# Loading k and v of batches 2 to 7 from ScalarE's DMA queue in place of SyncE's

## The chip, the cores and the metric

The kernel runs on one core of a Trainium2 chip. The metric is the device time of one execution in microseconds (us). The engines are named as in the profile: PE is TensorE's matmul side and PEld its weight loading, DVE is VectorE, ACT ScalarE, POOL GpSimd and SP SyncE. SP computes nothing here; it issues DMAs. A DMA that ACT issues stands in ACT's own instruction stream, between its activations, and goes into a queue of ACT's own; both queues are worked off by the same 16 DMA engines of the core.

## The reference

```python
# q, k, v: (8, 8, 576, 64) float32   g_norm: (64,)   w_in: (512, 2048)   w_out: (2048, 512)
kv = np.einsum('bhsd,bhse->bhde', k, v)
out = np.einsum('bhsd,bhde->bhse', q, kv)
rms = np.sqrt(np.mean(out * out, axis=-1, keepdims=True) + 1e-06)
x = (out / rms * g_norm).transpose(0, 2, 1, 3).reshape(8 * 576, 8 * 64)
h = x @ w_in
result = (h * np.cos(h)) @ w_out      # (4608, 512)
```

So for each batch and head, k and v make one 64 x 64 matrix `kv`; q times `kv`, normalized, gives the rows of `x`; and all 4608 rows go through two large matmuls with `h * cos(h)` between them.

## The kernel before

**Tiling.** The 4608 tokens are cut into 9 chunks of 512. A batch has 576 tokens, so chunks and batches overlap: batch b feeds chunk b - 1 and chunk b, roughly. Float32 matmuls are made of three passes over numbers split into a high and a low part (tiles ending in `hi` and `lo`, halves of `wi` and `wo`). Chunks 0 to 2 go through 48 steps, each with one 128-column block of `w_in` (12 matmuls into a `bank`) and the matching 128 rows of `w_out` (12 matmuls into four `acc` banks). Chunks 3 to 8 go in pairs through "quads" (`quad_part`, L1483): seven products of sums and differences take the place of eight, with weights read back from the DRAM tensors `wq` (for `w_in`) and `wod` (for `w_out`), which the kernel wrote earlier. In the profile those read-backs are the 512 KB loads `wo<-wq` and `wo<-wod`; `wo` is also the name of the buffers of w_out's split, in which they land.

**k and v.** Batches 0 and 1 (FRONT = 2) are loaded at the start in a way of their own. For each later batch b:

- `kv_loads` (L562) loads, for each of four pairs of heads, 512 of the 576 tokens of k into a tile `m` and of v into a tile `sg`, 256 KB each. `m` and `sg` come in five slots, which other stages use too.
- `over_loads` (L570) loads the last 64 tokens of all heads into `k_over` and `v_over`, 128 KB each.
- `kv_part` (L758) multiplies them on PE: the matmuls `bank<-sg,m` and `bank<-v_over,k_over`, pair after pair. ACT and DVE then split the result into `kv_w` (casts `kv_w<-bank` on ACT).
- `x_part` (L892) multiplies q by `kv_w` and normalizes. q comes through small DMAs `qb<-in_q_dram`, up to eight to a pair of heads.

That makes ten loads to a batch, of which six batches are concerned: 60 DMAs. Batch 2's are spread from 113 to 159 us; those of batches 3 to 7 come in bursts from 164, 213, 352, 364 and 423 us.

**What sets the order.** The class `Order` (L55) plays the whole program through when it is built, with costs and due times (`due`, L320, and the table `haste`, L327), and every instruction is recorded in the order in which it is chosen there; `Pinned` (L231) keeps that order on each engine. `dmas` (L520) takes 0.5 us of SP for an issue in this planner, whichever engine then issues, and allows eight DMAs in flight (`t_fly`, L513).

**Semaphores of DMAs.** In the built program the DMAs of all queues take eight semaphores in turn, `DMAHW0` to `DMAHW7`, and each DMA waits at its issue until the DMA before it on the same semaphore has landed, unless another wait already covers that. An engine that issues a DMA stands at that wait with all that follows in its stream.

**Places that the prediction speaks of.** The tiles `m`, `sg`, `k_over`, `v_over`; the weight loads `wo<-wq`; ACT's chain for h times cos(h) (`chain_part`, L1559: an activation into `ki`, DVE, a sine on ACT, DVE), and in the quads the adds that finish a bank (`add`, L1519; `snap`, L1513: copies `wi<-bank`).

Of the kernel before, what the change touches and what calls it, by code (L numbers as in the profile page):

```python
# [20 lines left out]
P = 128  # L21
# [164 lines left out]
def tile_kernel(  # L186
# [11 lines left out]
    B, H, S, D = q.shape  # L198
# [9 lines left out]
    SI = S // P  # L208
    ST = S - SI * P
# [31 lines left out]
    pe, act, dve, pool, sp = (Pinned(x) for x in (nc.tensor, nc.scalar, nc.vector, nc.gpsimd, nc.sync))  # L241
# [78 lines left out]
    def due(i):  # L320

        t = 24.0 + STEP * min(i, NS) + 2.0 * min(i, 11)
        first = max(0, min(i - NS, QUAD * NM))
        return t + 3.9 * first + 5.2 * max(0, i - NS - QUAD * NM)
# [136 lines left out]
    def put_off(*key):  # L461
        return haste.get(key, 0.0)
# [20 lines left out]
    def chunks_of(b):  # L483
        return [c for c in range(NCH) if any(x[0] == b for x in chunk_parts(c))]
# [26 lines left out]
    DMA_LAT, STORE_LAT = 1.3, 0.7  # L511
# [17 lines left out]
        yield "wait", landed  # L529
        return max(e.t for e in landed)  # L530

    def copies(out, in_, us, late=DMA_LAT):
        return us, late, lambda: sp.dma_start(out=out, in_=in_)

    def stores(out, in_, us):
        return copies(out, in_, us, STORE_LAT)
# [22 lines left out]
    def two(slot, shape, dtype, which):  # L559
        return at.tile(shape, dtype, name=f"{('m', 'sg')[which]}{slot}", bufs=1)  # L560

    def kv_loads(b, p):  # L562
        def pieces(slot):
            kv_tiles[b, p] = [two(slot, [P, 2, SI, D], F32, n) for n in range(2)], slot
            return [
                copies(t, src[b, 2 * p:2 * p + 2, 0:SI * P, :].rearrange("h (p i) d -> p h i d", i=SI), 0.74)
                for t, src in zip(kv_tiles[b, p][0], (k, v))]
        return pieces

    def over_loads(b):  # L570
        def pieces():
            return [
                copies(t[0:ST], src[b, :, SI * P:S, :].rearrange("h p d -> p h d"), 0.75)
                for t, src in ((k_over, k), (v_over, v))]
        return pieces

# [525 lines left out]
    def window(c):  # L1102

        if c < PLAIN:
            first = last_step[c - 2] + 1
            return first, begin[c] - first
        two_chunks, half = divmod(c - PLAIN, 2)
        first, n = (NS + QUAD * NM * (two_chunks - 1), QUAD * NM) if two_chunks else (begin[PLAIN - 1] - 4, NJ)
        return first + half * n // 2, n // 2
# [519 lines left out]
    for c in range(FRONT):  # L1629
        for p in range(NP):  # L1630
            t = due(begin[c]) - 32 + 3 * p if c else -100.0 + p
# [16 lines left out]
    for c in range(FRONT):  # L1648
        for p in range(NP):
            t = due(begin[c]) - 24 + 1 * p if c else -10.0 + 0.5 * p  # L1650
# [3 lines left out]
    for key in sorted(need, key=lambda x: (need[x], x)):  # L1654
        t = due(need[key]) - 14.0 + put_off("load", *key)
# [12 lines left out]
    for b in range(FRONT, B):  # L1668
        i, _ = window(chunks_of(b)[0])
# [8 lines left out]
    for c in range(FRONT, NCH):  # L1678
        first, n = window(c)
        for p in range(NP):  # L1680
            i, late = (first - 3 + p * (n - 1) // NP, 4) if c < PLAIN else (first + p * n // NP, 4 if c < PLAIN + 2 else 7)
# [9 lines left out]
    for j in range(NJ):  # L1691
        i = KEEP + j * (NS - KEEP - 8) // NJ
# [4 lines left out]
    for m in range(NM):  # L1697
        i = SUMS + m * (NS - SUMS - 6) // NM
# [46 lines left out]
```

## Time and profile before

| | |
|---|---|
| three timed runs | 840.77, 842.40 (median), 845.24 us |
| the profiled execution | 844.05 us, of which the span is 842.20 us |
| granted PE clock over the span | 0.997 |
| PE, PEld busy | 825.9 us (98%), 681.1 us (81%) |
| DVE, ACT, POOL busy | 613.8 us (73%), 498.2 us (59%), 227.6 us (27%) |
| moved by DMA | 181.20 MB, mean 215 GB/s |
| queue q1 (SP's) | 179.68 MB, 69.0% of the 16 engines' span |
| queue q10 (ACT's) | 0.72 MB, 0.2% |

How to read what is quoted: a row of a timeline gives start, duration, engine, line, operation, out<-in, shapes and a count (of merged instructions, with the duration of the whole stretch), and in brackets the engine's idle time before it and what ended that. Nearly all rows have line L239, the helper that records every instruction, so tiles' names tell them apart. "SPq" and "ACTq" are DMA issues by the sequencers of SP and ACT. A row of the DMA view gives the tile, the issuing queue, the count, the size, and the median time from issue to landing. A row of waits gives the waiting engine and tile, what it waited for, and us in total, times, longest. A row of stretches has the busy time of each engine with its count of instructions, then PE's clock, the DMA engines' mean busy share and GB/s. In the DMA view, a queue's row gives packets, MB and share of the 16 engines' time.

### The profile page before, as it was taken

Reading aid. Unit: us, or ns where it says so; the run is one execution under the profiler, and the core shown is the slowest. Engines: PE = TensorE matmul, PEld = TensorE weight load, DVE = VectorE, ACT = ScalarE, POOL = GpSimd, SP = SyncE. Lnnn points to the kernel's source line nnn. Section 1 sums busy time; section 2 is a strip of 40 time slices with the busy share of each in tenths; the row PEclk is TensorE's granted clock in tenths of the full one; section 3 lists DMA queues with packets and bytes.
Section 4 is the critical chain, followed back from the end, with each engine's and each line's share of the span. In section 5 each row is a group of like instructions: output and inputs, shape, how many; then the busy total and the mean of one; then the engine's idle time right before and its main releaser. Section 6 shows DMA issues by size and latency. Waiting matters only on the chain.

```text
span 842.2 us, 12749 instructions
## 1 busy us (share of the span) xinstructions
PE 825.9 (98%) x4424; PEld 681.1 (81%) x4424; DVE 613.8 (73%) x963; ACT 498.2 (59%) x974; POOL 227.6 (27%) x150
## 2 busy tenths in 40 slices
PE   8799999999999999999999999999999999999998
PEld 7678888888888887888887888888788888888886
DVE  3999994469598878669999968878899575444221
ACT  4879983445265565557786657767675464444321
POOL 3310034724427762010324620122438000000000
PEclk9999999999999999999999999999999999999999
DMA  9997535665765577598898767777557566763664
GB/s 301 299 399 275 176 113 190 194 176 155 236 184 189 152 205 269 175 335 254 267 278 233 216 190 183 211 248 201 176 200 240 175 195 191 229 215 105 223 206 145
DMA packets 150399, 181.20 MB, mean 215 GB/s; under 512 B 73920, under 2 KB 113600, under 8 KB 150336
## 3 DMA queue, kind: packets, MB, share of 16 engines
q1 hardware_dynamic: 149824, 179.68, 69.0%
q8 instruction: 35, 0.57, 0.3%
q10 hardware_dynamic: 512, 0.72, 0.2%
q14 instruction: 28, 0.23, 0.1%
HBM read 143.66 MB, written 36.70 MB: 214 GB/s over the span
## 4 chain that ended last, share of the span: by engine, by line
PE 81%; DMA 8%; DVE 5%; ACT 3%; issue 1%; SPq 1%; POOL 0%; DVEq 0%; ACTq 0%; POOLq 0%
PE bank L239 42%; PE acc L239 40%; DMA wi<-in_q_dram 2%; DVE r L239 1%; DMA wo<-wq 1%; DMA x<-slot 1%; DMA out_dram<-slot 1%; DMA wi<-in_v_dram 1%; DVE slot L239 1%; ACT slot L239 1%; DMA sg<-in_v_dram 1%; DMA slot<-part 1%; SPq L239 1%; DVE glo L239 1%; DMA wq<-slot 1%
## 5 line engine op out<-in xcount | busy, mean ns | idle before, releaser
L239 PE MATMUL acc<-wo,ghi 128*128 128x512 f32 x1152 | 355.7, 390 | 1.3 <-ACT slot L239 1.3
L239 PEld LDWEIGHTS acc<-wo,ghi 128*128 128x128 f32 x1152 | 215.4, 188 | 46.3 <-ACT slot L239 2.2
L239 PE MATMUL bank<-wi,wo 128*128 128x512 f32 (+2 forms) x1092 | 244.2, 380 | 4.2 <-DMA wo<-wq 2.0
L239 PEld LDWEIGHTS bank<-wi,wo 128*128 128x128 f32 (+2 forms) x1092 | 191.8, 185 | 46.8 <-DVE glo L239 2.4
L239 PE MATMUL acc<-wo,glo 128*128 128x512 f32 x576 | 224.3, 389 | 0.0
L239 POOL TENSOR_TENSOR rinv<-ms,mhalf 128x16 f32<-128x16 f32 (+1 forms) x36 | 97.2, 2703 | 228.9 <-DVE ms L239 228.5
L239 PEld LDWEIGHTS acc<-wo,glo 128*128 128x128 f32 x576 | 108.1, 188 | 23.0
L239 PE MATMUL bank<-xhi,wi 128*128 128x512 f32 x320 | 99.8, 393 | 0.2 <-DVE slot L239 0.2
L239 DVE TENSOR_TENSOR wi<-bank,wi 128x512 f32<-128x512 f32 x72 | 49.5, 687 | 44.4 <-PE bank L239 35.9
L239 DVE TENSOR_TENSOR glo<-wo,ghi 128x512 fp32r<-128x512 f32 x58 | 42.5, 732 | 46.1 <-ACT ghi L239 45.8
L239 ACT ACTIVATE ki<-wi 128x512 int32<-128x512 f32 x72 | 45.1, 627 | 42.4 <-DVE wi L239 33.7
L239 PEld LDWEIGHTS bank<-xhi,wi 128*128 128x128 f32 x320 | 58.8, 188 | 13.5 <-DVE r L239 0.8
L239 ACT CAST ghi<-wo 128x512 fp32r<-128x512 f32 x61 | 37.8, 619 | 48.4 <-PE acc L239 47.8
L239 ACT ACTIVATE ki<-bank 128x512 int32<-128x512 f32 x72 | 42.6, 591 | 34.2 <-PE bank L239 29.4
L239 PE MATMUL bank<-xlo,wi 128*128 128x512 f32 x160 | 62.4, 390 | 0.0
L239 ACT COPY wi<-bank 128x512 f32<-128x512 f32 x72 | 41.9, 583 | 24.2 <-PE bank L239 23.6
L239 ACT ACTIVATE wo<-wo 128x512 f32<-128x512 f32 x61 | 38.4, 630 | 26.1 <-DVE wo L239 25.8
L239 DVE TENSOR_TENSOR glo<-r,ghi 128x512 fp32r<-128x512 f32 x60 | 44.0, 733 | 13.1 <-ACT ghi L239 10.6
L239 ACT ACTIVATE r<-r 128x512 f32<-128x512 f32 x60 | 37.8, 630 | 20.1 <-DVE r L239 19.6
L239 DVE SCALAR_TENSOR_TENSOR r<-bank,ki 128x512 f32<-128x512 f32 x51 | 34.8, 683 | 19.9 <-ACT ki L239 19.4
L239 ACT CAST ghi<-r 128x512 fp32r<-128x512 f32 x60 | 37.1, 618 | 17.4 <-PE acc L239 16.0
L239 DVE TENSOR_TENSOR r<-r,bank 128x512 f32<-128x512 f32 x51 | 34.5, 678 | 8.5 <-ACT r L239 8.4
(175 smaller groups left out, 1071.6 us busy)
## 6 DMA issues: line engine op xcount, KB each, us to landing
wo<-wod SPq DMA_DIRECT2D x96, 512.0 KB, 3.4
wo<-wq SPq DMA_DIRECT2D x84, 512.0 KB, 4.0
out_dram<-slot SPq DMA_DIRECT2D x35, 256.0 KB, 3.4
wo<-in_moe_w_out_dram SPq DMA_DIRECT2D x16, 512.0 KB, 9.6
wi<-in_moe_w_in_dram SPq DMA_DIRECT2D x16, 512.0 KB, 9.9
wod<-wo SPq DMA_DIRECT2D x16, 512.0 KB, 4.1
wq<-wi SPq DMA_DIRECT2D x24, 256.0 KB, 3.5
m<-in_k_dram SPq DMA_DIRECT2D x24, 256.0 KB, 4.4
```

The source lines that it names most:

```text
L239: return lambda *a, **kw: tc.keep_in_program_order(f(*a, **kw))
```

## The change

`copies` can be told which engine issues, and the loads of `kv_loads` and `over_loads` name ACT:

```diff
-    def copies(out, in_, us, late=DMA_LAT):
-        return us, late, lambda: sp.dma_start(out=out, in_=in_)
+    def copies(out, in_, us, late=DMA_LAT, engine=None):
+        return us, late, lambda: (engine or sp).dma_start(out=out, in_=in_)
...
-                copies(t, src[b, 2 * p:2 * p + 2, 0:SI * P, :].rearrange("h (p i) d -> p h i d", i=SI), 0.74)
+                copies(t, src[b, 2 * p:2 * p + 2, 0:SI * P, :].rearrange("h (p i) d -> p h i d", i=SI), 0.74, engine=act)
...
-                copies(t[0:ST], src[b, :, SI * P:S, :].rearrange("h p d -> p h d"), 0.75)
+                copies(t[0:ST], src[b, :, SI * P:S, :].rearrange("h p d -> p h d"), 0.75, engine=act)
```

The planner still counts the issue on SP. The order of the instructions of PE, DVE and POOL is the same, and so is that of all that stays on ACT and on SP. What moves is where the 60 issues stand, and with it which DMA comes before which on the eight semaphores. The place that matters most below is batch 5, in the first quads.

On SP, this is the program before, from one weight load to the next; `wo_4010` and `wo_4042` are two of the 512 KB loads, between them stand batch 5's ten loads:

```order
L239 DMA wo_4010<-wq 128x1024 [waits DMAHW6_49,PE_49]
L239 DMA k_over<-in_k_dram 64x8x64 [waits DMAHW3_49]
L239 DMA m_4023<-in_k_dram 128x2x256 [waits DMAHW4_49]
L239 DMA m_4025<-in_k_dram 128x2x256 [waits DMAHW5_49]
L239 DMA m_4027<-in_k_dram 128x2x256
L239 DMA m_4029<-in_k_dram 128x2x256 [waits DMAHW7_49]
L239 DMA v_over<-in_v_dram 64x8x64 [waits DMAHW0_49]
L239 DMA sg_4024<-in_v_dram 128x2x256 [waits DMAHW1_49]
L239 DMA sg_4026<-in_v_dram 128x2x256 [waits DMAHW2_49]
L239 DMA sg_4028<-in_v_dram 128x2x256 [waits DMAHW3_49]
L239 DMA sg_4030<-in_v_dram 128x2x256 [waits DMAHW4_49]
L239 DMA wo_4042<-wq 128x1024 [waits DMAHW5_49,PE_49]
```

And the same place on SP with the change:

```order
L239 DMA wo_4010<-wq 128x1024 [waits DMAHW6_49,PE_49]
L239 DMA wo_4042<-wq 128x1024 [waits DMAHW0_49,PE_49]
L239 DMA wo_4070<-wq 128x1024 [waits DMAHW3_49,DMAHW1_49,PE_49]
L239 DMA wo_4082<-wq 128x1024 [waits DMAHW6_49,PE_49]
L239 DMA wo_4109<-wq 128x1024 [waits DMAHW2_49,DMAHW4_49,DMAHW0_49,PE_49]
L239 DMA wo_4129<-wod_146 128x1024 [waits DMAHW1_49,PE_49]
```

The ten loads are gone from SP, and the weight loads follow each other directly. Of their semaphores, some now belong to loads that ACT issues: `wo_4109` waits with DMAHW0 for `m_4029`.

On ACT, the same ten loads in the difference (+ is what the change adds), from the copy into `wi` on; the row of `k_over` stands just above it:

```order
+L239 DMA m_4023<-in_k_dram 128x2x256
+L239 DMA m_4025<-in_k_dram 128x2x256
+L239 DMA m_4027<-in_k_dram 128x2x256 [waits DMAHW7_49]
+L239 DMA m_4029<-in_k_dram 128x2x256 [waits DMAHW0_49]
 L239 ACTIVATE ki<-wi_3517 128x512 [waits DVE_49,Activation_49]
+L239 DMA v_over<-in_v_dram 64x8x64 [waits DMAHW1_49]
+L239 DMA sg_4024<-in_v_dram 128x2x256 [waits DMAHW2_49]
+L239 DMA sg_4026<-in_v_dram 128x2x256 [waits DMAHW4_49]
+L239 DMA sg_4028<-in_v_dram 128x2x256 [waits DMAHW6_49,DMAHW5_49]
 L239 ACTIVATE wo_3383<-wo_3383 128x512 [waits DVE_49]
+L239 DMA sg_4030<-in_v_dram 128x2x256 [waits DMAHW7_49]
 L239 ACTIVATE ki<-wi_3642 128x512 [waits Activation_49]
```

`sg_4026`, `sg_4028` and `sg_4030` now wait on ACT until `m_4023`, `m_4025` and `m_4027` have landed, and the activations into `wo_3383` and from `wi_3642` stand behind them.

## The prediction, made before the change was run

> **What bounds the kernel now.** I read the page first, then who waits for whom from 113 us on, where the moved loads begin, then the timelines of SP, PE and ACT around each batch of loads.
>
> ```profile
> span 842.2 us, 12749 instructions
> PE 825.9 (98%) x4424; PEld 681.1 (81%) x4424; DVE 613.8 (73%) x963; ACT 498.2 (59%) x974; POOL 227.6 (27%) x150
> ...
> PE bank L239 <- DMA wo<-wq: 2.0, 1, 2.0
> PE acc L239 <- ACT slot L239: 1.3, 2, 1.2
> PE bank L239 <- DVE r L239: 0.4, 2, 0.2
> ```
>
> TensorE works 98% of the span. From 113 us on it waits for five things, these three rows and two smaller ones, so for 2.0 + 1.3 + 3 x 0.4 = 4.5 us at most, and never for k or v. So nothing that frees SP can win more than 4.5 us. The 2.0 us wait is for a weight load that no moved load stands near, which leaves 2.5 us. A loss has no such bound: every microsecond by which ACT or a k/v load comes too late for TensorE is paid in full.
>
> **The change: ACT's time.** Sixty loads leave SP: 48 into m and sg, 12 into k_over and v_over.
>
> ```profile
> L239 SPq DMA_DIRECT2D m<-in_k_dram x24: 372/462/1702, 128.0 to 434.2; - x24
> L239 SPq DMA_DIRECT2D k_over<-in_k_dram x6: 601/604/717, 112.9 to 425.5; - x6
> ...
> 1.73 1.28 ACT L239 ACT_TABLE_LOAD   x1 [1.73 <-issue]
> 1.80 0.53 ACTq L239 DMA_DIRECT2D gcol<-in_g_norm_dram  x1
> ```
>
> An issue takes SP 0.46 us (0.60 for the two "over" tiles). The one issue of ACT's shown here took 0.53, much the same, so ACT's sequencer gets 48 x 0.46 + 12 x 0.60 = 29 us more, beside 498 us of busy time in 842. It ran at 1.80, inside the table load of 1.73 to 3.01: one issue between two activations hides behind the first of them. I take nothing for a single one (from 0 up to 0.46 if not hidden), and 0.5 for each further one in a row.
>
> **The change: the early batches (2, 3, 4) and 7.** Batches 3, 4 and 7 are loaded far ahead of their matmuls; batch 4 stands for them, with the last pairs of batch 2.
>
> ```profile
> 213.29 2.80 SPq L239 DMA_DIRECT2D m<-in_k_dram  x3
> 262.02 0.69 PE L239 MATMUL bank<-sg,m 128*64 128x64 f32 x16 [0.17 <-DVE r L239]
> ...
> sg<-in_v_dram SPq DMA_DIRECT2D x1, 256.0 KB, 4.4
> 159.41 0.62 ACT L239 CAST sg<-slot 128x512 fp32r<-128x512 f32 x1 [0.83 <-POOL slot L239]
> 164.51 0.64 PE L239 MATMUL bank<-sg,m 128*64 128x64 f32 x16
> ```
>
> With 262.02 - 213.29 = 49 us to go, batch 4's landings cannot matter. ACT's delay can: two or three issues in a row, between activations, put it 0.5 to 1.5 us back, mostly caught up in its idle time. I choose 0.2 us for batches 3 and 4 together (0 to 0.7) and, as ACT is busier there, 0.4 us for batch 7 (0 to 1.0). Batch 2's last v load now stands behind a cast that waits for POOL until 159.41. Issued at 159.45, it lands at 159.45 + 4.4 = 163.9, 0.6 before its matmul at 164.51: nothing, and up to 0.5 if the cover fails.
>
> **The change: batch 5, where it is decided.** Here the loads are issued at 352 and multiplied at 363.
>
> ```profile
> 351.73 0.32 SPq L239 DMA_DIRECT2D wo<-wq  x1
> 352.10 0.60 SPq L239 DMA_DIRECT2D k_over<-in_k_dram  x1
> 352.75 2.15 SPq L239 DMA_DIRECT2D m<-in_k_dram  x4
> 354.94 0.61 SPq L239 DMA_DIRECT2D v_over<-in_v_dram  x1
> 355.60 2.36 SPq L239 DMA_DIRECT2D sg<-in_v_dram  x4
> 357.49 0.47 SPq L239 DMA_DIRECT2D sg<-in_v_dram  x1
> 358.06 3.56 SPq L239 DMA_DIRECT2D wo<-wq  x4
> k_over<-in_k_dram SPq DMA_DIRECT2D x1, 128.0 KB, 4.5
> sg<-in_v_dram SPq DMA_DIRECT2D x1, 256.0 KB, 5.9
> wo<-wq SPq DMA_DIRECT2D x1, 512.0 KB, 6.6
> wo<-wq SPq DMA_DIRECT2D x1, 512.0 KB, 8.0
> 363.24 0.69 PE L239 MATMUL bank<-sg,m 128*64 128x64 f32 x16
> 365.04 0.64 PE L239 MATMUL bank<-sg,m 128*64 128x64 f32 x16
> 368.58 0.61 PE L239 MATMUL bank<-wi,wo 128*128 128x512 f32 x2
> 356.00:360.00 4.00, 4.00 (x20) 3.30 (x19) 3.26 (x6) 1.84 (x4) 0.00 (x0) 1.00 1.10 310
> ```
>
> The DMA rows give issue to landing. k_over lands at 352.10 + 4.5 = 356.6, the last sg (the row of 357.49 shows it alone) at 357.49 + 5.9 = 363.4. The first of the four 512 KB weight loads behind them lands at 358.06 + 6.6 = 364.7, the fourth, whose issue of 0.32 ends the stretch at 358.06 + 3.56 = 361.62, at 361.30 + 8.0 = 369.3: one every (369.3 - 364.7) / 3 = 1.5 us. The last row is a stretch of 4 us; its last but one column, a DMA share of 1.10, says that the engines are full, so landings follow the queue's order. The last pair of k and v is multiplied at 365.04: its cover is 1.6 us. The first weight load is used only at 368.58, 3.9 us after it lands. SP's single queue put the urgent loads ahead of the patient ones.
>
> The change takes that order away. What SP now issues after 351.73 is the next weight load.
>
> ```profile
> SPq L239 <- DMA m<-in_k_dram: 1.4, 2, 1.1
> 350.63 10.64 PE L239 MATMUL bank<-wi,wo 128*128 128x512 f32 x46
> q1 hardware_dynamic: 383, 0.38, 53.8%
> q10 hardware_dynamic: 191, 0.40, 51.8%
> ```
>
> Before, two of those loads waited for k loads to land (first row, SP's waits from 351.9 to 362). Their other wait is for TensorE to leave a weight buffer: two products of six matmuls at 10.64 / 46 = 0.23 us, so about 2.8 us after 351.73, at 354.5. So the first goes out some 3.5 us earlier, ahead of most v loads. The last two rows are 3 to 5 us, the only time when both queues have work: q1 (SP's) moves 0.38 MB, q10 (ACT's) 0.40 MB. Two full queues share evenly. While k and v go on (6.8 us from first to last landing), SP's queue gets as much again, as far as it has loads: three for certain (due at about 354.5, 357.3 and 360), a fourth once the fourth m load has landed. By landing order the last sg comes at 363.4 + n x 1.5: 367.9 with n = 3, 369.4 with n = 4. TensorE is ready at 365.04, so it loses 2.9 or 4.4 us. I take 3.4, three loads and a third of the fourth; the ends are 0.9 (only one gets by: 363.4 + 1.5 = 364.9, but then ACT's own lateness counts, below) and 4.4.
>
> [...]
>
> ACT is late there too. Each DMA waits until the one eight before it has landed; on ACT, that holds back the activations behind it.
>
> ```profile
> m<-in_k_dram SPq DMA_DIRECT2D x2, 256.0 KB, 4.5
> m<-in_k_dram SPq DMA_DIRECT2D x1, 256.0 KB, 5.8
> 357.80 0.61 ACT L239 ACTIVATE ki<-wi 128x512 int32<-128x512 f32 x1
> 361.33 0.69 DVE L239 TENSOR_TENSOR wo<-wo,bank 128x512 f32<-128x512 f32 x1
> ```
>
> The m loads need 4.5 to 5.8 us. The third went out on SP at about 353.9 (third of four in 2.15 us from 352.75); on ACT, behind a cast and a copy, I estimate 354.7, and a landing near 359.6; only then may the last sg go, and behind it stands the activation that began at 357.80: it starts at 360.0, 2.2 late. It heads a chain through DVE and ACT that ended at 361.33 + 0.69 = 362.0 and that TensorE needs at 363.24, so 1.2 of it is covered and 1.0 is lost, up to 2.5 if sharing holds that m load up by another 1.5. It ends in the same stretch of TensorE as the missing sg, so the two do not add: the larger, 3.4, counts. Without sharing this 1.0 is what is left.
>
> **The change: batch 6.** Loaded at 364 to 376 and multiplied far later. With TensorE 3.4 us late, what ACT waits for has mostly landed when it asks: 0.
>
> **Sum.** 3.4 + 0.2 + 0.4 = 4.0 us. The profiled execution took 844.05 us (span 842.20), so 848.05 for it; the median of the three runs is 842.40, 1.65 below, so I forecast 842.4 + 4.0 = **846.4 us**. A difference under 0.5%, 4.2 us, can hardly be told from none in this kernel: the three runs reach from 840.77 to 845.24.
>
> **The rivals.**
> *The cover holds.* Sharing costs the v loads little, one weight load gets by, and ACT's lateness of 1.0 is all. For it: the weight loads may start more slowly than I think. Against it: 53.8% and 51.8% on the two queues. With batch 7's share or without, 1.0 to 1.5 us: 843.5 us.
> *ACT's waits run on through batch 6 (the other side: clearly slower).* There, two copies and a chain of casts stand behind an sg load that, by the eight-apart rule, waits for a q load.
>
> ```profile
> 366.33 0.88 SPq L239 DMA_DIRECT2D qb<-in_q_dram  x1
> qb<-in_q_dram SPq DMA_DIRECT2D x1, 40.0 KB, 8.0
> 370.14 0.59 ACT L239 COPY wi<-bank 128x512 f32<-128x512 f32 x1 [0.71 <-PE bank L239]
> ```
>
> It landed at 366.33 + 8.0 = 374.3, so with an issue of 0.4 the copy of 370.14 would start at 374.8, 4.6 late. It decides once that exceeds the copy's cover before TensorE; if SP's loads shift along with TensorE, so that batch 5's 3.4 gives no relief, and there is no cover, it is 4.0 + 4.6: 851.0 us. For it: SP's own queue now waits for ACT's loads. Against it: SP, rid of ten issues, sends that q load no later.
> *Faster.* SP's freed time removes what is left of TensorE's waits: 842.4 - 2.5 = 839.9 us. Against it: those waits are for ACT and DVE, not for SP.
>
> **How the numbers follow.** The forecast's case (2.5 to 6 us lost) has 0.48, the cover that holds 0.27, the run-on 0.20, faster 0.05. The forecast's case alone is 844.9 to 848.4. To hold 8 in 10 the range goes down over the second case, less the scatter of a median, to 842.0, and up to 850.0, leaving out the worst of the run-on. Slower by over 0.5% (above 846.6) is the run-on's 0.20 and 0.22 of the forecast's 0.48: 0.42. Faster by over 0.5% needs more than the 2.5 us there are: 0.03 for scatter. The same: 0.55.
>
> **What would show it.** In the profile of the changed kernel: the weight load wo<-wq issued near 354.5 and not at 358; TensorE idle for some 3 us before one of the bank<-sg,m groups near 365, released by a DMA from in_v; the sg loads of batch 5 taking 7 to 10 us; activations at 357 to 361 some 2 to 4 us late. The forecast is wrong if that stop is under 1 us (the v loads kept their place), or if TensorE stops again at 370 to 385 behind ACT.

## The result, and the profile after

| | before | changed |
|---|---|---|
| median of six runs | 842.42 us (840.77 to 845.24) | 851.29 us (849.86 to 852.83) |
| profiled execution | 844.05 us | 852.83 us |
| ratio of the times | | 1.0101, 95% interval 1.0087 to 1.0115 |

The change costs 8.9 us. The forecast was 846.4 us with a range up to 850.0: the direction and the place were right, the size was not.

First the head of the page of the changed kernel, and of TensorE's waits from 113 us on the four rows that are new or longer (waiting engine and tile, what it waited for, us in total, times, longest).

```profile
span 851.0 us, 12722 instructions
PE 829.0 (97%) x4424; PEld 682.5 (80%) x4424; DVE 614.4 (72%) x963; ACT 497.9 (59%) x974; POOL 228.4 (27%) x150
...
PE bank L239 <- DMA sg<-in_v_dram: 3.2, 2, 2.2
PE bank L239 <- DVE wo L239: 1.4, 1, 1.4
PE bank L239 <- DVE sg L239: 0.9, 2, 0.6
PE bank L239 <- DVE wi L239: 0.7, 1, 0.7
```

TensorE waits for a v load, which it never did before, and it is also 829.0 - 825.9 = 3.1 us longer busy with the same 4424 matmuls. The stops for v are all at batch 5, and the matmuls there take 3.2 us longer; what they gain and lose elsewhere cancels to about nothing. The timelines of SP and ACT there:

```profile
351.18 10.21 SPq L239 DMA_DIRECT2D wo<-wq  x5
362.80 0.32 SPq L239 DMA_DIRECT2D wo<-wod  x1
...
352.83 2.31 ACTq L239 DMA_DIRECT2D m<-in_k_dram  x4
355.93 3.30 ACTq L239 DMA_DIRECT2D sg<-in_v_dram  x3
359.28 0.63 ACT L239 ACTIVATE wo<-wo 128x512 f32<-128x512 f32 x1 [3.41 <-DMA m<-in_k_dram]
359.57 0.38 ACTq L239 DMA_DIRECT2D sg<-in_v_dram  x1
359.99 0.63 ACT L239 ACTIVATE ki<-wi 128x512 int32<-128x512 f32 x1
```

SP now issues its weight loads without a break, five wo<-wq from 351.18 to 361.39 and a wo<-wod at 362.80. ACT stands 3.41 us at the issue of an sg load until an m load has landed, with the activations behind it. In the DMA view, first the last sg load and the wo<-wod load, each looked up alone (last column: us from issue to landing), then the two queues from 363 to 368 us (packets, MB, share of the 16 engines' time):

```profile
sg<-in_v_dram ACTq DMA_DIRECT2D x1, 256.0 KB, 10.7
wo<-wod SPq DMA_DIRECT2D x1, 512.0 KB, 7.2
...
q1 hardware_dynamic: 435, 1.53, 75.1%
q10 hardware_dynamic: 520, 0.50, 28.4%
```

The sg load lands at 359.57 + 10.7 = 370.3 and the wo<-wod load at 362.80 + 7.2 = 370.0: all five loads that SP issued behind 351.18 got past it. The numbers of packets are not far apart here, but SP's average 3.5 KB (1.53 MB in 435) and ACT's 1.0 KB (0.50 MB in 520), so SP got three times the bytes. What TensorE did then, from its timeline and from the table of stretches (the third column from the end is its granted clock):

```profile
364.20 0.69 PE L239 MATMUL bank<-sg,m 128*64 128x64 f32 x16 [1.44 <-DVE wo L239]
368.06 1.12 PE L239 MATMUL bank<-sg,m 128*64 128x64 f32 x16 [2.20 <-DMA sg<-in_v_dram]
370.42 1.12 PE L239 MATMUL bank<-sg,m 128*64 128x64 f32 x16 [1.02 <-DMA sg<-in_v_dram]
373.13 1.05 PE L239 MATMUL acc<-wo,ghi 128*128 128x512 f32 x2
375.22 0.61 PE L239 MATMUL acc<-wo,ghi 128*128 128x512 f32 x2
...
366.00:368.00 2.00, 0.00 (x0) 0.00 (x0) 1.97 (x4) 1.46 (x3) 0.00 (x0) 0.96 1.03 400
368.00:370.00 2.00, 1.33 (x20) 1.15 (x20) 0.74 (x2) 0.00 (x0) 0.00 (x0) 0.50 0.62 139
372.00:374.00 2.00, 2.00 (x6) 1.52 (x6) 1.10 (x2) 1.04 (x3) 0.00 (x0) 0.50 0.44 137
```

Three stops, 1.44 + 2.20 + 1.02 = 4.7 us, the first behind ACT and DVE, the other two for v. After the two microseconds without a matmul the clock is granted at half, and the same two matmuls that take 0.61 us at 375 take 1.05 at 373.

As the instructions of TensorE stand in the same order in every kernel here, the same matmul can be looked up in two traces. The table gives how much later than in the first profile of the kernel before TensorE stands after a stretch than ahead of it; the columns name the times in that profile. The kernels are those of the experiments below.

| us gained (-) or lost (+) between | start, 45 | 110, 245 (batches 2 to 4) | 330, 345 | 345, 382 (batches 5, 6) | 432, 470 (batch 7) | end |
|---|---|---|---|---|---|---|
| changed | +0.3 | +1.4 | -2.6 | **+7.9** | +1.6 | +8.8 |
| changed, second profile | +0.3 | +0.4 | -3.0 | **+7.8** | +1.9 | +7.4 |
| before, second profile | +1.2 | +0.2 | -2.4 | 0.0 | 0.0 | -0.3 |
| batch 5 on ACT | +0.5 | -0.6 | -3.6 | **+8.4** | -0.5 | +4.4 |
| all but batch 5 on ACT | +1.7 | 0.0 | -2.3 | +1.0 | +3.5 | +3.8 |
| batch 5 on POOL | +5.0 | 0.0 | -2.6 | 0.0 | -0.5 | +2.5 |
| batch 5 on ACT, weights in 1 KB runs | +2.1 | +0.1 | -2.8 | **+4.4** | -1.0 | +3.1 |
| k of batch 5 on ACT, three profiles | -0.5, +5.0, +0.4 | -0.8, -0.2, -0.1 | -2.8, -2.7, +0.1 | **+2.5, +2.7, +2.8** | -0.6, +0.2, -0.3 | -2.0, +5.3, +2.8 |
| v of batch 5 on ACT | +1.3 | -0.5 | -3.0 | **+7.1** | -0.6 | +4.8 |
| batch 7 on ACT | +2.0 | +0.1 | -2.9 | 0.0 | +0.9 | +0.5 |
| batches 2, 3, 4, 6 on ACT | +0.2 | +0.3 | -2.4 | +0.2 | -0.6 | -2.4 |

The first column and the third are scatter of single executions: the program is the same up to some 350 us in the kernels that move batch 5 or 7 alone (with POOL up to 331 us, where its first load stands). The third column is negative because the first profile of the kernel before had a stop there that hardly any other had (below). The column of batch 5 repeats within 0.1 us for the changed kernel and within 0.3 for k alone, and carries the result.

### The profile page after: what moved, and what is told of

Same layout as the page of the kernel before. It is cut to its first block, busy times and chain, and to the rows that moved or that the text cites. A ratio compares the mean times of both kernels' runs of the same rounds, so it can differ in the third digit from the quotient of the medians.

```text
span 851.0 us, 12722 instructions
## 1 busy us (share of the span) xinstructions
PE 829.0 (97%) x4424; PEld 682.5 (80%) x4424; DVE 614.4 (72%) x963; ACT 497.9 (59%) x974; POOL 228.4 (27%) x150
## 4 chain that ended last, share of the span: by engine, by line
PE 77%; DMA 8%; DVE 6%; ACT 4%; POOL 2%; issue 1%; SPq 1%; ACTq 0%; DVEq 0%; POOLq 0%
PE acc L239 39%; PE bank L239 38%; DMA sg<-in_v_dram 2%; DMA wq<-m 2%; DVE r L239 1%; DMA m<-in_k_dram 1%; DMA x<-slot 1%; POOL m L239 1%; POOL rinv L239 1%; DVE sg L239 1%; ACT slot L239 1%; DVE glo L239 1%; DMA wq<-wi 1%; DMA qb<-in_q_dram 1%; ACT ghi L239 1%
## 5 line engine op out<-in xcount | busy, mean ns | idle before, releaser
L239 DVE TENSOR_TENSOR glo<-r,ghi 128x512 fp32r<-128x512 f32 x60 | 44.4, 739 | 13.2 <-ACT ghi L239 10.6
```

Source lines behind the costliest of these rows:

```text
L239: return lambda *a, **kw: tc.keep_in_program_order(f(*a, **kw))
```

## The experiments

The theory after the result: TensorE's loss is made at batch 5, where (a) SP's weight loads, in runs of 4 KB, pass ACT's k and v loads, in runs of 1 KB, because the two queues share by packets and not by bytes (a guess that fits 435 packets to 520 above, and that the runs below test), and (b) the granted clock halves behind the stops (0.50 at 368 to 374 above). The rivals: ACT's waits for landings hold its activations back, and that makes TensorE late; or the sixty issues cost ACT a little everywhere.

Medians in us, each kernel beside the kernel before on the same chip. The ratio is worked out from all runs and is not that of the two medians; where it is turned into us below, it is taken times the median before. The second looks at the end are single executions and not in the table:

| kernel | median | before, same chip | ratio, 95% interval |
|---|---|---|---|
| batch 5 on ACT | 850.86 | 843.72 | 1.0092 (1.0067 to 1.0118) |
| all but batch 5 on ACT | 845.14 | 843.72 | 1.0032 (1.0012 to 1.0052) |
| batch 5 on POOL | 844.74 | 843.72 | 1.0025 (1.0008 to 1.0042) |
| batch 5 on ACT, weights in 1 KB runs | 846.48 | 843.72 | 1.0044 (1.0025 to 1.0062) |
| k of batch 5 on ACT | 846.60 | 843.35 | 1.0034 (1.0012 to 1.0056) |
| v of batch 5 on ACT | 849.52 | 843.35 | 1.0069 (1.0052 to 1.0086) |
| batch 7 on ACT | 844.46 | 843.35 | 1.0017 (1.0000 to 1.0034) |
| batches 2, 3, 4, 6 on ACT | 844.53 | 843.35 | 1.0012 (0.9994 to 1.0029) |

### Batch 5 alone on ACT

```diff
-    ..., 0.74, engine=act)
+    ..., 0.74, engine=act if b == 5 else sp)
...
-    ..., 0.75, engine=act)
+    ..., 0.75, engine=act if b == 5 else sp)
```

> Only batch 5's ten loads go through ACT's queue; the other fifty stay on SP. Theory (packets in turn): the DMA engines take a packet of 4 KB from SP's weight loads for every packet of 1 KB from ACT's k and v loads, so batch 5's last sg lands near 370 in place of 363, and nearly all of the loss is made there: two stops of TensorE at bank<-sg,m of 2 and 1 us, one of 1.4 us just ahead of them for ACT, and some 5 us at half the clock behind them; 842.4 + 8.0 = 850.4 us (849 to 851.5). Rival (spread): ACT's own time for the 60 issues costs some 1.5 us in each of six batches; 843.9 us here.

Its ratio of 1.0092 is some 7.8 us (5.7 to 10.0; the medians differ by 7.1), nearly the whole loss, and a sixth of the loads makes it. TensorE's waits in its trace:

```profile
PE bank L239 <- DMA sg<-in_v_dram: 2.5, 3, 1.7
PE bank L239 <- DVE wo L239: 1.6, 1, 1.6
```

The stops are 2.5 + 1.6 = 4.1 us, and 8.4 us are lost in the stretch: the other half is the slow clock (granted 0.50 from 364 to 372). The rival that spreads the cost is out.

### All but batch 5 on ACT

```diff
+    ..., engine=sp if b == 5 else act)
```

> All but batch 5's loads go through ACT's queue. Theory (packets in turn): near 363 TensorE does not stop and its clock stays full; what is left are the small stops that the changed kernel shows at 163, 231, 442 and 459, 0.7 + 0.5 + 0.7 + 0.6 = 2.5 us: 844.9 us (843.5 to 846). Rival (spread): five sixths of the loss are left, 849.8 us.

845.14 us, 1.0032 times the kernel before: as the theory had it. Its profile is of one of the longer executions, 847.87 us. In the stretch of batches 5 and 6 it loses 1.0 us, at one stop of 0.8 us behind DVE's work on `kv_w`. The rest is at batch 7. Timelines of ACT and PE, and the k_over load in the DMA view:

```profile
426.52 0.65 ACTq L239 DMA_DIRECT2D k_over<-in_k_dram  x1
434.08 0.62 ACTq L239 DMA_DIRECT2D v_over<-in_v_dram  x1
435.47 0.63 ACT L239 ACTIVATE ki<-wi 128x512 int32<-128x512 f32 x1 [3.44 <-issue]
...
437.48 2.93 PE L239 MATMUL bank<-wi,wo 128*128 128x512 f32 x6 [2.60 <-DVE wi L239]
...
k_over<-in_k_dram ACTq DMA_DIRECT2D x1, 128.0 KB, 7.5
```

The k_over load, in runs of 256 bytes, lands at 426.52 + 7.5 = 434.0 (on SP's queue, in the kernel before, the same load took 3.3 us); ACT's issue of v_over stands until then, the activation behind it starts 3.44 us after ACT fell idle, and TensorE stops 2.60 us. In the two profiles of the changed kernel the same stretch costs less, 1.6 and 1.9 us.

### Batch 5 from POOL's queue

```diff
+    ..., engine=pool if b == 5 else sp)
```

> Batch 5's ten loads are issued by POOL, which has next to nothing to do there; ACT and SP otherwise as in the kernel before. Theory (packets in turn): a queue of its own loses to SP's 4 KB packets whoever issues, so TensorE still stops for sg, 3 us or more with the slow clock behind it, while the stop of 1.4 us for ACT's lateness is gone: 846 to 850 us. Rival (ACT's waits: the activations behind the loads that wait for landings are what makes TensorE late): 842.4 to 843.5 us. If POOL's issues take longer than SP's 0.46 us, the last sg is later by that as well, which the trace shows.

844.74 us, neither the theory's 846 to 850 nor the rival's 842.4 to 843.5, and no stop near 363 at all. That does not speak for the rival, since the premise was not met. Timelines of POOL and SP, and POOL's queue in the DMA view of the whole run:

```profile
346.18 0.71 POOL L239 DMA_DIRECT2D v_over<-in_v_dram  x1 [4.92 <-issue]
352.62 0.72 POOL L239 DMA_DIRECT2D sg<-in_v_dram  x1 [0.45 <-issue]
...
347.31 14.64 SPq L239 DMA_DIRECT2D wo<-wq  x6
...
q0 software_dynamic: 736, 2.36, 0.8%
```

TensorE ran 3.1 us later here than in the first profile, so POOL's last sg at 352.62 is some 8 us earlier than SP's at 357.49 had been. POOL has little to do and comes to these issues early, ahead of most of SP's weight loads. Its queue is of another kind, too (`software_dynamic` in the row): 736 packets for 2.36 MB are 3.2 KB on average, not 1 KB. So this run has loads that are issued earlier and in larger packets, and they were in time; which of the two did it stays open, and (a) against ACT's waits is undecided. What the ratio has over 1 (0.7 to 3.5 us) the profile does not explain. The next three decide.

### Batch 5 on ACT, with the passing weight loads in runs of 1 KB

```diff
-            ... copies(w.bitcast(F32), wq[:, s:s + 2], 1.5) ...
+            part = wq[:, s - 2:s + 2, 0, :] if 11 <= t <= 14 else wq[:, s:s + 2]
+            ... copies(..., part, 1.5) ...
```

> As the kernel with only batch 5 on ACT, but the four weight loads wo<-wq that go past it read their 512 KB in runs of 1 KB (half rows of other weights, so the products of those four loads are made with wrong numbers) and not of 4 KB. Theory (packets in turn): with packets of one size the two queues get equal bytes, the last sg lands at 365 to 367.5 and not near 370, and TensorE's stops for sg shrink from 3.2 us to 0 to 1.5: 844 to 847 us. Rival (equal bytes whatever the packets, or ACT's waits): no change against the kernel with only batch 5 on ACT.

The four loads read half rows of twice as many weight rows, so the bytes are as many and the products made with them are of other numbers. The queues from 361 to 366 us, here (first two rows) and in the changed kernel, where TensorE stands within 0.1 us of the same place when batch 5's loads begin (next two), and the one large stop of TensorE in this kernel:

```profile
q10 hardware_dynamic: 922, 0.85, 55.2%
q1 hardware_dynamic: 852, 0.86, 53.8%
...
q1 hardware_dynamic: 365, 1.36, 68.0%
q10 hardware_dynamic: 627, 0.61, 35.6%
...
365.55 1.07 PE L239 MATMUL bank<-sg,m 128*64 128x64 f32 x16 [2.75 <-DVE wo L239]
```

With 1 KB runs on both sides the bytes are equal, where SP had more than twice ACT's. The last sg lands at 360.92 + 6.7 = 367.6 in place of 370.3, behind two of the weight loads in place of five. TensorE has no stop for sg left, in place of 2.5 us; the loss in the stretch falls from 8.4 to 4.4 us, the time from 850.86 to 846.48. So it is shown that here the length of the runs decides which queue gets the bytes. One packet for one packet is not: the counts are 852 to 922 here, but 365 to 627 in the changed kernel, and 435 to 520 in it two microseconds later. And the stop behind ACT and DVE grew from 1.6 to 2.75 us, with 1.6 us of slow clock behind it (granted 0.50 from 366 to 368): the theory without ACT's waits is not the whole. That stop also covers what is left of the other: without it TensorE would have come to its last group of `bank<-sg,m` near 365.0 - 0.5 = 364.5 (the time before, and the 0.5 us by which it runs earlier here), some 3 us ahead of the last sg, by this estimate.

### Only k, and only v, of batch 5 on ACT

```diff
+    for t, src, e in zip(kv_tiles[b, p][0], (k, v), (act if b == 5 else sp, sp))]    # k alone
...
+    for t, src, e in zip(kv_tiles[b, p][0], (k, v), (sp, act if b == 5 else sp))]    # v alone
```

> Of batch 5 only k goes through ACT's queue; its v loads stay on SP, ahead of the weight loads. Theory (packets in turn): k shares the engines mostly with v, in packets of the same 1 KB and both are needed together, and no weight load goes by; the last sg lands within about 1 us of the 363.4 of before, TensorE does not stop for sg: 0 to 1.5 us over the kernel before on the same chip. Rival (ACT's waits: any load in ACT's stream that waits for a landing makes the activations late): 3 us or more over it, with a stop of TensorE behind DVE and ACT.

With k alone the theory's 0 to 1.5 us was wrong, and the rival's 3 us with a stop behind DVE and ACT was right: 2.9 us by the ratio. The interval alone (1.0 to 4.7) would not tell them apart; the stop does, in all three profiles. Timelines of ACT and PE, and a stretch behind the stop:

```profile
349.49 5.18 ACTq L239 DMA_DIRECT2D m<-in_k_dram  x4
354.77 0.63 ACT L239 ACTIVATE ki<-wi 128x512 int32<-128x512 f32 x1 [4.72 <-DMA m<-in_k_dram]
...
356.78 3.02 PE L239 MATMUL bank<-wi,wo 128*128 128x512 f32 x12 [2.16 <-DVE wi L239]
...
358.00:360.00 2.00, 2.00 (x10) 1.64 (x9) 1.27 (x3) 1.56 (x3) 0.00 (x0) 1.00 1.06 395
```

Four issues take ACT 5.18 us, as they wait for landings; the activation behind them is 4.72 us late and TensorE stops 2.16 us at its bank. There is no stop for sg.

> Of batch 5 only v goes through ACT's queue; its k loads stay on SP. Theory (packets in turn): v stands alone against SP's weight loads of 4 KB packets; the last sg lands 3 to 6 us later than before, TensorE stops for sg as in the kernel with all of batch 5 on ACT, and the clock halves behind it: 5 to 8 us over the kernel before on the same chip. Rival (the loss needs both k and v on ACT, or comes from the issues in number): about half of the 7.1 us that all of batch 5 cost.

With v alone, the waits of TensorE:

```profile
PE bank L239 <- DMA sg<-in_v_dram: 3.2, 2, 2.3
PE bank L239 <- DVE wo L239: 0.5, 1, 0.5
```

3.2 us for sg and 0.5 behind ACT, 7.1 us lost in the stretch with the slow clock (granted 0.50 from 368 to 372), 5.8 us by the ratio. So there are two mechanisms, each seen nearly alone: the lost order (v alone) and ACT's waits (k alone). Their 5.8 and 2.9 us make 8.7, beside 7.8 for both at once.

### Batch 7 alone, and batches 2, 3, 4 and 6

```diff
+    ..., engine=act if b == 7 else sp)                  # the one kernel
+    ..., engine=sp if b in (5, 7) else act)             # the other
```

> Only batch 7's loads go through ACT's queue. Theory: its k_over, in packets of 256 bytes, loses most to the weight loads' 4 KB packets and lands 6 to 7.5 us after its issue; v_over's issue on ACT waits for that, and the activation behind it (32.08 to 35.47 in the two kernels, counted from 400) makes TensorE stop 0.7 to 2.6 us near 435: 1 to 4 us over the kernel before on the same chip. Rival (batch 7 cost nothing of its own, the stops there are scatter): 0 to 0.5 us.

1.0017, some 1.4 us (0.0 to 2.9). Its one stop near 435:

```profile
434.95 1.65 PE L239 MATMUL bank<-wi,wo 128*128 128x512 f32 x6 [0.82 <-DVE wi L239]
```

A cost of about 1 us at batch 7 is likely; the interval just reaches no cost.

> Batches 2, 3, 4 and 6 go through ACT's queue. Theory: there the loads have time to spare, and only ACT's lateness is left: stops of TensorE near 163, 231 and 371 of 0.5 to 0.8 us each: 0.5 to 2 us over the kernel before on the same chip. Rival (ACT's time for forty issues is paid in full): 40 x 0.46 = 18 us of ACT's sequencer would show as 4 us or more.

1.0012, interval from 0.9994: within what was expected, and not told apart from nothing. Of the three stops of 0.5 to 0.8 us that were expected, its profile (of its shortest execution, 841.59 us) shows none over 0.3 us. The forty issues are not paid in full, which would have been 4 us or more.

### Second looks: k alone, the kernel before, the changed kernel

> A second look at the kernel with only batch 5's k on ACT, whose times spread from 841.5 to 849.9 us while its profile was of an execution of 842.0, with a stop of 2.2 us and the clock at 1.00 behind it. Theory (the clock): in a longer execution the same stop stands near 357 and the granted clock is halved for some 4 us behind it, 1.5 to 2 us more of TensorE's busy time; in another short one it stays at 1.00. Rival: the spread comes from stops for sg, which the first profile happened not to have.

> The same kernel a third time, with the same two readings: a longer execution has either a halved clock behind the stop near 357 (the clock) or a stop for sg near 362 (rival).

The stop ahead of that matmul in the second profile and the third:

```profile
363.00 3.04 PE L239 MATMUL bank<-wi,wo 128*128 128x512 f32 x12 [2.34 <-DVE wi L239]
```

```profile
361.42 3.04 PE L239 MATMUL bank<-wi,wo 128*128 128x512 f32 x12 [2.47 <-DVE wi L239]
```

Both readings of the spread fail: the clock stays at 1.00 behind the stop and there is no stop for sg in either. The stop itself is steady, 2.2 to 2.5 us. The spread comes from elsewhere, by the table: in the first 45 us (-0.5, +5.0, +0.4) and at 335 (-2.8, -2.7, +0.1), places ahead of all that this kernel changes. There the clock does have a part in it: the second profile has 10.2 us at half clock in the first 45 us, and TensorE is busy 4.9 us longer there; the first has none (mean granted clock over the span 0.993 and 1.000).

> The kernel before, profiled once more. Theory: the stop of 2.0 us for wo<-wq at 335.5 and the slow clock behind it are chance (the eight other profiles have 0.0 to 0.8 there), so it is under 1 us here and the clock stays at 1.00; near 363 TensorE does not stop. Rival: the stop belongs to the kernel before, and 3.5 us of it are a gain that the change brings.

The only stop of TensorE between 330 and 345, from its timeline:

```profile
336.93 3.00 PE L239 MATMUL bank<-wi,wo 128*128 128x512 f32 x12 [1.20 <-DMA wo<-wq]
```

1.20 us and not under 1, but the clock stays at 1.00 and the stretch costs 2.4 us less than in the first profile. Over all profiles the stop for this load is 0.0 to 2.1 us, also among kernels that are the same up to there. It is chance, not a gain of the change. Near 363 there is no stop.

> The changed kernel, profiled once more. Theory: near 363 to 371 again a stop of 1 to 2 us behind ACT and DVE, stops for sg of 2.5 to 4 us together, and some 5 us of half clock; at 442 again a stop, between 0.5 and 3 us. Rival: these were the chance of one execution, and the loss is spread otherwise.

The three longest of TensorE's waits:

```profile
PE bank L239 <- DMA sg<-in_v_dram: 3.3, 2, 2.1
PE bank L239 <- DVE sg L239: 2.0, 2, 1.7
PE bank L239 <- DVE wo L239: 1.9, 1, 1.9
```

Batch 5 again: 1.9 behind ACT, 3.3 for sg, and 7.8 us in the stretch. Batch 7's stop is at another place than expected, 1.7 us at `bank<-sg,kv_w` (458.09) and none at 442.

## Why the prediction was wrong

**What bounds the kernel, and what the change does to the order.** Right. SP's next weight load was issued at 353.96, forecast near 354.5; three more followed at 356.68, 358.73 and 361.08, of which two were forecast at 357.3 and 360. TensorE stopped for batch 5's v, whose sg loads took 7.0 to 10.7 us for a forecast 7 to 10.

**"Two full queues share evenly."** This step failed. It rested on the rows at 3 to 5 us, with 0.38 MB and 0.40 MB. At 361 to 366 it was 1.36 to 0.61 MB, at 363 to 368 1.53 to 0.50, and with packets of one size 0.86 to 0.85. Where the runs differed, the longer got more: at 361 to 366 the packets average 3.7 KB on SP's queue (1.36 MB in 365) and 1.0 KB on ACT's (0.61 MB in 627). The early rows do not go by the length of the runs (383 packets of 1.0 KB and 191 of 2.1 KB, at equal bytes), and why stays open. In the sum, n was 3 and a third; it was 5, the wo<-wod load included, which the count of passing loads had left out. With n = 5 the prediction's formula gives 363.4 + 5 x 1.5 = 370.9; the last sg landed at 370.3.

**"... the two do not add: the larger, 3.4, counts."** This failed too. ACT's lateness itself was forecast closely: the third m load was to land near 359.6 and the activation to start at 360.0; it started at 359.99. But its stop, 1.4 and 1.9 us in the two profiles for the 1.0 forecast (up to 2.5), comes ahead of the first group of bank<-sg,m and the stops for sg come after the second: 1.44 + 3.22 = 4.7 us in place of 3.4.

**The missing term: the clock.** No step had it, and so it stood at nothing without a reason. In the stretch of batch 5 the changed kernel loses 7.9 us, of which 4.7 are stops; the other 3.2 are matmuls at half clock (in its second profile 5.2 and 2.6). The cost stood in the trace of before, whose wait of 2.0 us for a weight load the prediction shows, without the stretch behind it. These are stretches of the kernel before (first two rows) and of the one with k alone:

```profile
332.56:335.98 3.42, 1.45 (x7) 0.93 (x6) 3.01 (x5) 2.50 (x5) 0.00 (x0) 1.00 0.89 289
335.98:339.39 3.41, 3.41 (x10) 2.62 (x9) 0.20 (x2) 1.31 (x3) 0.00 (x0) 0.50 0.29 102
...
352.98:356.40 3.42, 1.64 (x8) 1.02 (x6) 0.97 (x2) 0.87 (x2) 0.00 (x0) 1.00 1.09 365
356.40:359.81 3.41, 3.03 (x13) 2.54 (x14) 2.59 (x5) 2.28 (x5) 0.00 (x0) 1.00 1.08 389
```

In the traces the granted clock changes only at the ends of steps of 3.41 us (before: at 335.98, at 339.39 and, 147 steps on, at 841.15), whose place in the program differs from execution to execution. Inside the program it is halved for one step, as here behind 335.98, for two (6.83 us, the changed kernel, in both profiles) or for three (10.24 us, batch 5 on ACT). Which stops do it goes by how much of the stop falls into one step: TensorE's idle time was 3.42 - 1.45 = 1.97 us in the first row, and the next step ran at half; the stop of 2.16 us with k alone falls into two steps, with 1.78 and 0.38 us, and both its steps and the next one ran at full clock. Cut into such steps, the fourteen profiles have half the clock behind every full-clock step of the program with 1.9 us of idle time or more (1.97 above, 2.11 in the changed kernel, 2.75 with the weights in 1 KB runs), behind none with less than 1.6 (the longest before is 1.54), and either in between (1.65 before and 1.77 changed left it full).

So a stop's length alone does not tell: 1.97 us halved the clock, 2.16, 2.34 and 2.47 with k alone did not. Why the clock goes by such steps no run shows.

**The other batches.** 0.2 for batches 3 and 4 and 0.4 for batch 7 were taken. The two profiles show 1.4 and 0.4 us for batches 2 to 4, and 1.6 and 1.9 for batch 7, above the upper end of 1.0 there. The path at batch 7 was not the one named (issues in a row) but ACT's wait for the landing of k_over: in the kernel with all but batch 5 on ACT as shown above, and in the first profile of the changed kernel v_over's issue, at 439.10, also comes right behind the landing of k_over (433.15 + 5.9), ahead of a stop of 0.7 us at 442.5. In its second profile the stop was another, at 458.

**The sum again.** With measured sizes: 4.7 in stops at batch 5, 3.2 of clock, some 1 for batches 2 to 4 and 1.7 for batch 7 make 10.6 us; timed were 8.9 (1.0087 to 1.0115: 7.3 to 9.7). The 1.7 between them is less than what single executions differ by at places that the change does not touch (table, first and third column); where it belongs is not shown.

**The rivals.** "ACT's waits run on through batch 6" named 851.0 us, close to the 851.29, for another reason: TensorE did not stop between 372 and 385 in the changed kernel. So its nearness to the time is luck. The mechanism, ACT's waits for landings, was real, but at batches 5 and 7.

## What to carry to other kernels

A load that moves to a second queue loses its place ahead of the loads left on the first (here the last sg landed at 370.3 in place of 363.4). Where the engines are full, ask which bytes now pass it, and look at the length of the runs: here the queue with 4 KB runs got two to three times the bytes of the one with 1 KB (1.36 to 0.61 MB, 1.53 to 0.50). On an engine that computes, each issue that may wait for a landing is a wait for everything behind it (here 3.4 to 5 us of ACT). And price a stop of a busy TensorE with the half clock that can follow: here 3.2 us on top of 4.7.

## What the runs showed of the hardware that was not expected

- Two queues with work for all engines shared by the length of the runs: 1.36 to 0.61 MB (365 to 627 packets) and, two microseconds later, 1.53 to 0.50 MB (435 to 520) with 4 KB against 1 KB; 0.86 to 0.85 MB (852 to 922) with 1 KB on both. At 3 to 5 us two queues did not: 0.38 to 0.40 MB at 383 to 191 packets.
- The granted clock went in steps of 3.41 us. It was 0.50 for one to three of them behind a full-clock step in which TensorE had stood 1.9 us or more, and full behind each with less than 1.6; so a stop of 1.97 us had it, and one of 2.47 us, split between two steps (0.92 and 1.55), had not. Behind the stops of batch 5 this cost 3.2 us beside the 4.7 of the stops.
- The first 45 us of the program differ by up to 5.5 us between executions of kernels that are the same there (-0.5 to +5.0 in the table), about as much as the times of one kernel spread. In both executions with +5.0, 10.2 us ran at half clock up to 47 us (mean granted clock over the span 0.994 with POOL, 0.993 in the second profile with k alone).
